# Scaling the turned features by the modulation in place of the projection weights, with a new order of the opening, row-split runs for the output projection's remainder and a last product in halves

## The chip, the cores and the metric

The kernel runs on one core of one Trainium2 chip. The metric is the device time of one execution in microseconds (us); medians over several executions are given with their lowest and highest value. The profile is one execution taken by the hardware profiler; its "span" runs from the first to the last instruction and is some 2 us shorter than the device time. The engines are called TensorE (PE in the profile, PEld for its weight loads), VectorE (DVE), ScalarE (ACT), GpSimd (POOL) and SyncE (SP, which issues DMA here).

## The reference

One layer on 2048 rows of 576 features: linear attention with 32 heads of 18, then a feed-forward part of width 4608, both behind a layer norm that is scaled and shifted by a modulation computed from a vector `c`.

```python
mod = (silu(c) @ w_mod).reshape(1, 6, 1, -1)
sa, ca, ga, sb, cb, gb = ...                     # six rows of 576
h = layernorm(x) * (1 + ca) + sa
x = x + ga * A(h)
h = layernorm(x) * (1 + cb) + sb
x = x + gb * (relu(h @ w1) @ w2)

def A(x):
    q, k, v = split(x @ wqkv)                    # 32 heads of 18
    phi_q = concat(softmax(q @ w_phi), softmax(-q @ w_phi))
    phi_k = concat(softmax(k @ w_phi), softmax(-k @ w_phi))
    kv, z = phi_k^T v, sum(phi_k)
    return (phi_q kv / (phi_q z + 1e-6)) @ wo
```

## The kernel before

Time passes in two parts. The **opening** computes the modulation, multiplies ("folds") the K and Q weights with `w_phi`, projects 16 row tiles to K, V and Q, sums kv, and runs attention for the first two tiles. Its instructions are written in one hand-searched list of short words. `Ka0` is four of the five chunks of the K projection of tile 0, `sa`/`sp` are statistics, `fs` and `ws` scale folded or value weights by `1 + ca`, `tp` forms a third of a weight difference for the feed-forward part, `nu`/`nO` are attention's numerator and its division, `W` is the output projection.

```python
ORDER = """
Z11 sx sd rp sc FK ca Z2 fs0 fsr frr fra2 sh frd4 fra0 fra1 bn1 fs3 bn0 fs1 Z1 fra3 shc sa0 wsd2 KR:0 fsd4 fs2
sp0 bn2 T0:2 VR:1 KRh bn3 Tc0 Ka0:2 KRd sa2 wsd1 ...
... Q3:0 tp0 wo4 qt1 kz Q4:1 eQ3 wo2 sq2
tp2 Q5:2 eQ4 sq3 tp1 wo3 nu0:3 eQ5 Q6:0 sq4 nO0 ...            # cut
"""
```

The **blocks**, eight of two row tiles each, run the feed-forward part: the first layer in three groups, then the second layer as seven products on sums and differences of halves (fewer multiplications than eight). Attention for the next block is slipped in: numerator in the first layer, output projection, norm and a DMA transposition in the second.

```python
def wo_mm(t, pr, add_x):
    for k in range(2):
        if add_x:                                 # the residual, through an identity matmul
            pe.matmul(pr[:, k, 0:HD], lhsT=ident[:, 0:P], rhs=x_sb[:, t, k * HD:(k + 1) * HD], start=True, stop=False)
        for ci in range(NC):                      # 5 chunks; the last has 64 real rows
            pe.matmul(pr[:, k, 0:HD], lhsT=oT[:, t % 2, ci, :], rhs=wo_sb[:, ci, k * HD:(k + 1) * HD], ...)

def l1_rest(js, u, hb):                           # half-height products, two row halves side by side
    for n, j in enumerate(js):
        for hf in range(2):
            b0 = 64 * hf
            pe.matmul(..., lhsT=w1b[b0:b0 + 64, j * P:(j + 1) * P], rhs=hb[b0:b0 + 64, 4, :], ...)

def l2(b, hooks):                                 # cut
    prod(Y, A12, B21, al, True)
    fin(t, 0, Y, 0)                               # VectorE add, GpSimd gate and residual
    if b > 0:
        pool.tensor_tensor(out=A12, in0=A12, in1=U2, op=ALU.subtract)
    ...
    prod(Z, A12, B22, al)                         # last block
    dve.tensor_tensor(out=yt[:, 0, :], in0=PS[:, Z, 0:HD], in1=gb_row[:, HD:D], op=ALU.mult)
    dve.tensor_tensor(out=x_sb[:, t, HD:D], in0=yt[:, 0, :], in1=z, op=ALU.add)
    sp.dma_start(outf[rows, HD:D], x_sb[:, t, HD:D])

def in_l1(g, u):
    if (g, u) in ((0, -1), (0, 1)):               # softmax of the query tile, and its transposition
        q_fin(q)
    if (g, u) in ((1, 2), (2, 1)):
        num_mm(t, pr); num_o(t, pr); turn_dma(oT[:, t % 2], o_sb[:, t % 2, :])

def in_l2(pos):
    if pos in (1, 4):                             # wo_mm, residual, statistics
        ...
    if pos in (2, 6):                             # normalize to xn, transpose by DMA into h2
        ln2_rs(t); ln2_apply(t, None); turn_dma(h2[...], xn[:, t % 2, :])
    if pos == 12:                                 # scale and shift the next block's features
        for ci in range(NC):
            dve.tensor_scalar(out=hb[:, ci, :], ...)
```

The softmax here doesn't subtract the row's maximum and nothing guards it: scores larger than these inputs give would overflow.

## Time and profile before

| | before |
|---|---|
| median of the first runs | 392.11 us (391.75 to 392.55, 3 runs) |
| execution that was profiled | 392.93 us, span 390.7 us |
| first feed-forward product | 93.52 us |
| each of the seven block periods | 37.05 us |
| last matmul ends | 386.79 us, tail 3.91 us |

The times of a profile are to be read from the span's start. Two markers carry most of this document: the start of the first feed-forward product (the length of the opening) and the distance between first products of neighbouring blocks (the period). What remains is the tail, from the end of the last matmul to the end of the span. The execution that was profiled was slower than every other run of that first set.

### The profile page before, as it was taken

The page shows a single profiled execution, that of the slowest core. Times are in us where ns is not written, and L with a number is a line of the kernel's source. Part 1 is how long each engine was busy: PE and PEld are TensorE (multiplying, and loading weights), DVE is VectorE, ACT ScalarE, POOL GpSimd, SP SyncE. Part 2 cuts the span into 40 slices and gives each one's busy share as a digit, 9 for nine tenths or more (in the row PEclk, how much of TensorE's full clock was granted, in tenths as well). Part 3 has the DMA queues.
Part 4 walks back from the last instruction along what each step waited for, and adds up shares of the span by engine and source line. Part 5 has one row for each costly group of instructions (what it writes and reads, how often), then busy time and mean ns, then how long its engine had stood idle before and what let it go on. Part 6 is the DMA issues. An engine that isn't in the chain of part 4 may idle for free.

```text
span 390.7 us, 8908 instructions
## 1 busy us (share of the span) xinstructions
PE 383.8 (98%) x3693; PEld 311.7 (80%) x3693; DVE 244.3 (63%) x452; ACT 157.9 (40%) x360; POOL 142.3 (36%) x199
## 2 busy tenths in 40 slices
PE   8999999999999999999999999999999999999995
PEld 4778888878887888788888878887888788878874
DVE  0889998854879746573755567458555664653221
ACT  1798779699531233124213510531143123312510
POOL 2155858741101510740164045306510641072045
PEclk9999999999999999999999999999999999999999
DMA  7999739795732151125313311450143124010001
GB/s 291 418 420 403 274 133 354 178 306 161 189 65 35 47 121 20 35 61 109 35 27 83 80 35 32 107 65 19 47 93 35 24 69 51 18 34 33 3 0 32
DMA packets 49515, 44.36 MB, mean 114 GB/s; under 512 B 39361, under 2 KB 42050, under 8 KB 48706
## 3 DMA queue, kind: packets, MB, share of 16 engines
q1 hardware_dynamic: 49186, 43.59, 39.6%
q8 instruction: 29, 0.48, 0.5%
q10 hardware_dynamic: 288, 0.19, 0.2%
q14 instruction: 12, 0.10, 0.1%
HBM read 27.97 MB, written 6.49 MB: 88 GB/s over the span
## 4 chain that ended last, share of the span: by engine, by line
PE 86%; POOL 6%; ACT 2%; DVE 2%; DMA 2%; issue 1%; SPq 0%; POOLq 0%; DVEq 0%; ACTq 0%
PE PS L683 33%; PE PS L742 29%; PE PS L274 9%; PE PS L410 5%; PE PS L690 5%; POOL wo_sb L637 2%; PE PS L235 2%; PE PS L391 1%; ACT RT L279 1%; POOL RH L754 1%; DMA gatd<-gt 1%; PE PS L324 1%; POOL RT L291 1%; DMA ga_row<-gatd 1%; DVE st L240 1%
## 5 line engine op out<-in xcount | busy, mean ns | idle before, releaser
L683 PE MATMUL PS<-h,R 128*128 128x256 bf16 x1152 | 133.5, 273 | 0.0
L683 PEld LDWEIGHTS <-R 128*128 128x128 bf16 x1152 | 109.8, 98 | 17.5 <-issue 5.1
L742 PEld LDWEIGHTS <-RH 128*128 128x128 f16 x864 | 84.5, 98 | 21.8
L728 POOL TENSOR_TENSOR yt<-yt,gb_row 128x288 f32<-128x288 f32 x23 | 16.8, 731 | 167.0 <-DVE yt L727 167.0
L742 PE MATMUL PS<-R,RH 128*128 128x288 bf16 (+1 forms) x576 | 75.6, 286 | 0.0
L697 ACT ACTIVATE RH<-PS 128x256 f16<-128x256 f32 x72 | 27.7, 384 | 114.0 <-PE PS L690 107.4
L699 DVE SCALAR_TENSOR_TENSOR RH<-PS,RH 128x256 f16<-128x256 f32 x72 | 30.1, 419 | 68.2 <-ACT RH L697 68.2
L279 ACT ACTIVATE RT<-PS,rs 128x576 bf16<-128x576 f32 x64 | 43.0, 750 | 7.5 <-PE PS L274 7.1
L698 ACT ACTIVATE RH<-PS 128x512 f16<-128x512 f32 x72 | 42.9, 595 | 7.8 <-PE PS L683 6.5
L746 ACT ACTIVATE RS<-PS 128x288 f32<-128x288 f32 x24 | 9.9, 411 | 75.9 <-PE PS L742 75.9
L742 PE MATMUL PS<-RT,RH 128*128 128x288 f16 x288 | 37.9, 286 | 0.0
L274 PE MATMUL PS<-RH,R 116*128 116x288 bf16 x240 | 31.8, 286 | 0.5 <-ACT RH L631 0.5
L754 POOL TENSOR_TENSOR RH<-RH,RT 128x2304 f16<-128x2304 f16 x7 | 31.8, 4548 | 0.0
L274 PE MATMUL PS<-RH,RT 116*128 116x288 bf16 x240 | 31.7, 286 | 0.0
L274 PEld LDWEIGHTS <-R 116*128 116x128 bf16 x240 | 22.9, 98 | 6.4 <-issue 0.7
L274 PEld LDWEIGHTS <-RT 116*128 116x128 bf16 x240 | 22.7, 98 | 5.5
L420 DVE TENSOR_SCALAR xn<-x_sb,mv,rs 128x576 bf16<-128x576 bf16 (+1 forms) x28 | 22.4, 842 | 7.3 <-ACT rs L415 7.3
L729 POOL TENSOR_TENSOR x_sb<-yt,x_sb 128x288 bf16<-128x288 f32 x31 | 22.8, 737 | 5.9 <-DVE yt L725 4.1
L240 DVE BATCH_NORM_STATS2 st<-x_sb 128x6 f32<-128x288 bf16 x60 | 24.2, 445 | 0.5
L410 PE MATMUL PS<-wo_sb,oT 128*128 128x288 bf16 x160 | 22.6, 286 | 0.2 <-POOL wo_sb L637 0.2
L284 DVE TENSOR_REDUCE Rk<-RT 128x64 f32<-128x1152 bf16 x16 | 21.2, 1332 | 1.4 <-ACT RT L279 1.4
L284 DVE TENSOR_REDUCE Rq<-RT 128x64 f32<-128x1152 bf16 x16 | 21.5, 1342 | 0.0
(115 smaller groups left out, 414.2 us busy)
## 6 DMA issues: line engine op xcount, KB each, us to landing
R<-in_w1a_dram SPq DMA_DIRECT2D x4, 1152.0 KB
eqd<-RT SPq DMA_DIRECT2D x14, 288.0 KB, 5.8
RT<-eqd SPq DMA_DIRECT2D x14, 288.0 KB, 2.7
R<-in_w2a_dram SPq DMA_DIRECT2D x3, 864.0 KB, 10.4
R<-in_w2b_dram SPq DMA_DIRECT2D x2, 1296.0 KB, 10.9
out_dram<-x_sb SPq DMA_DIRECT2D x15, 144.0 KB, 3.3
RT<-in_xT_dram SPq DMA_DIRECT2D x2, 640.0 KB
x_sb<-in_xk_dram SPq DMA_DIRECT2D x3, 288.0 KB
```

Source lines behind the costliest of these rows:

```text
L240: dve.bn_stats(out=s[:, hf, :], in_=x_sb[:, t, hf * HD:(hf + 1) * HD])
L274: pe.matmul(pr[:, k, 0:HD], lhsT=xt(t, ck), rhs=w[0:R, ck, k * HD:(k + 1) * HD], start=(ck == 0), stop=(ck == NC - 1))
L279: act.activation(out=E.rearrange("p (b h s e) -> p b h s e", b=2, s=2, e=DH)[:, :, :, s, :], in_=pr[:, :, 0:HD].rearrange("p b (h e) -> p ...
L284: dve.tensor_reduce(out=Rr, in_=E.rearrange("p (c e) -> p c e", e=DH), axis=AXX, op=ALU.add)
L410: pe.matmul(pr[:, k, 0:HD], lhsT=oT[:, t % 2, ci, :], rhs=wo_sb[:, ci, k * HD:(k + 1) * HD], start=(ci == 0 and not add_x), stop=(ci == NC ...
L683: pe.matmul(PS[:, 2 * u + hf, n * 256:n * 256 + 256], lhsT=w1a[:, ci, jj * P:(jj + 1) * P], rhs=hb[:, ci, :], start=(n == 0 and ci == 0), ...
L697: act.activation(out=A11[:, j, :], in_=lo[:, :, 0, :], func=ACT.Relu)
L698: act.activation(out=A2[:, j, :, :], in_=PS[:, 2 * u + 1, :].rearrange("p (n s f) -> p n s f", n=2, s=2), func=ACT.Relu)
L699: dve.scalar_tensor_tensor(out=U3[:, j, :], in0=lo[:, :, 1, :], scalar=0.0, in1=A11[:, j, :], op0=ALU.max, op1=ALU.subtract)
L729: pool.tensor_tensor(out=x_sb[:, t, c], in0=y, in1=x_sb[:, t, c], op=ALU.add)
L742: pe.matmul(PS[:, bank, 0:HD], lhsT=am[:, j, :], rhs=bm[:, j, :], start=first and j == 0, stop=(j % 9 == 8), skip_group_check=True)
L754: pool.tensor_tensor(out=A12, in0=A12, in1=U2, op=ALU.subtract)
```

## The change

The intent is fourfold. (1) In the opening the weights stay raw; instead the transposed features are multiplied by `1 + ca`, pair by pair, on three engines, so the first K projection waits for less; the loads and the whole order are searched anew. The residual is added by VectorE and not by identity matmuls. (2) In blocks with index 2 and more, attention moves to an earlier place, and the output projection's fifth chunk runs as two half-height products side by side, next to other such products. (3) GpSimd's subtraction for the last product moves to VectorE, except in the block with index 1. (4) The very last product is computed in halves of 144 columns.

```diff
+    def x_scale(t, eng):                         # in place of f_scaled, wv_scale, FQs
+        for ck in range(NC):
+            v, f = xt(t, ck, 2), ca1[0:R, ck:ck + 1]
+            act.activation(out=v, in_=v, func=ACT.Copy, scale=f)      # or VectorE; GpSimd all at once
-        "W": lambda i: wo_mm(i, at["W", i], True), "lb": lambda i: ln2_bn(i, at["W", i]), ...
+        "W": lambda i: wo_mm(i, at["W", i]), "xr": lambda i: add_res(i, at["W", i]), "lb": lambda i: bn(1, i), ...
 ... (the ORDER list and the order of the loads are new throughout)
         fin(t, 0, Y, 0)
         if b > 0:
-            pool.tensor_tensor(out=A12, in0=A12, in1=U2, op=ALU.subtract)
+            (pool if b == 1 else dve).tensor_tensor(out=A12, in0=A12, in1=U2, op=ALU.subtract)
 ... (last block)
-        prod(Z, A12, B22, al)
-        dve.tensor_tensor(out=yt[:, 0, :], in0=PS[:, Z, 0:HD], in1=gb_row[:, HD:D], op=ALU.mult)
-        dve.tensor_tensor(out=x_sb[:, t, HD:D], in0=yt[:, 0, :], in1=z, op=ALU.add)
+        for i, bank in enumerate((Z, 0)):
+            c, g = slice(i * H4, (i + 1) * H4), slice(HD + i * H4, HD + (i + 1) * H4)
+            for j in al:
+                pe.matmul(PS[:, bank, c], lhsT=A12[:, j, :], rhs=B22[:, j, c], ...)
+            dve.tensor_tensor(out=yt[:, 0, c], in0=PS[:, bank, c], in1=gb_row[:, g], op=ALU.mult)
+            dve.tensor_tensor(out=x_sb[:, t, g], in0=yt[:, 0, c], in1=yl[:, c], op=ALU.add)
+    def wo_rest(t, pr):
+        for k in range(2):
+            b0 = 64 * k
+            pe.matmul(pr[:, k, 0:HD], lhsT=oT[b0:b0 + 64, t % 2, 4, :], rhs=wo_sb[b0:b0 + 64, 4, ...], ...)
 ... (in_l1, in_l2: blocks 0 and 1 keep the old places, from index 2 on)
+            if (g, u) in ((0, 0), (0, 2)):
+                attend(t0 + u // 2)
+            if g and u == "rest":
+                wo_rest(t0 + g - 1, pair(3))
+            if g and u == 0:
+                wo_full(t, pair(3)); add_res(t, pair(3)); bn(1, t)
+            if b > 1 and pos in (4, 10) or b == 1 and pos == 8:
+                q_next(t0 + 2 + pos // 8)         # softmax of a query tile, now in the second layer
```

## The prediction

> **What bounds the kernel now.** I read the page first: shares by engine, then the chain of waits.
>
> ```profile
> span 390.7 us, 8908 instructions
> PE 383.8 (98%) x3693; PEld 311.7 (80%) x3693; DVE 244.3 (63%) x452; ACT 157.9 (40%) x360; POOL 142.3 (36%) x199
> ...
> PE 86%; POOL 6%; ACT 2%; DVE 2%; DMA 2%; issue 1%; SPq 0%; POOLq 0%; DVEq 0%; ACTq 0%
> ```
>
> TensorE is busy for 98% of the span and carries 86% of the last chain. But matmuls overlap, so busy time is no proof that the rate is full. I therefore went to the chain in order of time for one feed-forward block (there are eight, 37.05 us apart) and compared pieces with counts.
>
> ```profile
> 130.73 3.06 PE PS L683 x28
> 133.79 0.76 PE PS L690 x12
> 134.55 5.35 PE PS L683 x48
> 139.90 0.76 PE PS L690 x12
> 140.66 2.29 PE PS L683 x20
> 142.95 0.38 PE PS L391 x10
> ...
> 149.81 1.19 PE PS L742 x9
> 151.00 1.23 PE PS L410 x10
> 152.22 3.31 PE PS L742 x27
> 155.53 1.23 PE PS L410 x10
> 156.76 11.03 PE PS L742 x90
> ```
>
> First number start, second length. 90 second-layer products take 11.03 us, 122.6 ns each; 28 first-layer products 3.06 us, 109 ns; the 12 half-height ones 0.76 us, 63 ns each, because they run in pairs. All pieces touch. Adding the pieces of one block gives 3 x 6.11 (first layer) + 2 x 0.38 (attention numerator) + 2 x 1.23 (output projection) + 126 x 0.1226 = 37.0 us, which is the period. So the blocks, from 93.5 us to the end, have no gap: only fewer or cheaper matmuls help there.
>
> The opening is different. The TensorE timeline before 24 us has waits and fill-in matmuls on zeros:
>
> ```profile
> 12.58 0.38 PE L235 MATMUL PS<-zero 128*128 128x512 bf16 x1
> 12.79 0.38 PE L251 MATMUL PS<-siluc,R 116*116 116x1 bf16 x5
> 13.04 0.38 PE L235 MATMUL PS<-zero 128*128 128x512 bf16 x1
> 14.16 1.40 PE L268 MATMUL PS<-R,RS 116*100 116x288 bf16 x10 [0.75 <-DVE RS L614]
> ...
> 19.62 0.27 PE L577 MATMUL PS<-ident,sc 128*100 128x128 bf16 x2 [0.26 <-DVE RH L481]
> ...
> 23.41 1.39 PE L274 MATMUL PS<-RH,R 116*128 116x288 bf16 x10 [0.49 <-ACT RH L631]
> ```
>
> The brackets name who was waited for. The shift copy (L614) sits behind statistics on VectorE; the correction row (L481) behind weight scalings. VectorE is busy 10.2 of the 10.6 us from 14.16 to 24.72. The first K projection starts at 16.74. Summing real work from 14.16 to 93.52 at its pitch (480 projections x 0.1226 = 58.9, 24 output products 2.9, rows 2.5, folds 1.7, kv 5.8, gates and modulation 2.6, transposes and numerators 2.8) gives 77.2 us of 79.4, so some 2.2 us of gaps, half before 24.72. Last, the end of the kernel:
>
> ```profile
> 377.93 4.54 POOL L754 TENSOR_TENSOR RH<-RH,RT 128x2304 f16<-128x2304 f16 x1
> ...
> 386.89 0.46 DVE L777 TENSOR_TENSOR yt<-PS,gb_row 128x288 f32<-128x288 f32 x1 [1.75 <-PE PS L742]
> 387.49 0.46 DVE L778 TENSOR_TENSOR x_sb<-yt 128x288 bf16<-128x288 f32 x1
> 387.98 0.33 SPq L779 DMA_DIRECT2D out_dram<-x_sb  x1
> ```
>
> The last matmuls end at about 386.8; two VectorE operations of 0.46 and the store follow. GpSimd's late chain (the 4.54 us subtraction, then gate and residual) ends at 387.46 and holds the second one by about 0.1.
>
> **What the Trainium skill says.** "TensorE: Matmul & The Clock Gate", section "Wait — 56ns, not 53.3ns?", gives a warm back-to-back pitch of N / 2.4 GHz + 2.5 ns: 122.5 ns for 288 columns, 109.2 for 256. The trace agrees (122.6 and 109). "TensorEngine Tiling (Array Packing)", section "Key Properties", says that independent row tiles can run in parallel and that changing the tiling mode drains the engine. The trace agrees with the first: twelve half-height products are six slots of 0.107 = 0.64 us, and take 0.76; the 0.12 left is what I take for the switch. So adding a pair to a run that is already split should cost one slot and no switch. "VectorE: DVE Perf Modes", section "The perf-mode tier table (the rule you actually need)", puts a 16-bit tensor-scalar from on-chip memory at four elements a cycle and anything from PSUM at two at most; here 116x576 scaled from SBUF took 366 ns and the 116x504 scaling from PSUM 0.73 us, so it agrees.
>
> **The change, part by part.**
>
> 1. Feature scaling in place of weight scaling, with the new order. Off VectorE go five value-weight scalings at a pitch of 0.31 (1.55 us), one 0.65 and one 0.44 fold scaling; off ScalarE four fold scalings of 0.69 and five query-fold ones of 0.73 (6.4 us). New: eight pairs of tiles must be scaled, five 116x256 slices each on VectorE (two pairs) and ScalarE (three), one 116x1280 multiply on GpSimd (three). From the 335 ns row for 128x256 on VectorE I take at most 0.3 a slice, 1.3 us a pair. ScalarE: the 4x256 copy's 0.38, 1.7 to 1.9 us a pair. GpSimd: 576 elements took 1.17 to 1.27, so 1280 about 2.7. These lie mostly beside TensorE. What counts is the start: the K projection no longer waits for the correction rows; its first four chunks need raw folded weights, scaled features and the modulation scale. The new load order delivers in sequence at about 0.4 MB/us (725 + 288 + 725 + 725 + 320 KB plus the small ones), so the features land near 11.4; scale ready at 9.5, copies done near 12, shift products done near 12.9. Ka0 can start near 13 instead of 16.74, but rows, fill-ins and the two last chunks then follow. Laying them end to end, the pair of K tiles is complete at about 18.3 instead of 19.2, and four later projections end near 22.9 instead of 24.6. I take 1.4 us saved at the start, and 0.4 of the later gaps.
>
> 2. Residual added on VectorE, not by identity matmuls: 4 x 0.1226 = 0.49 us of TensorE gone. VectorE pays 2 x 0.75 instead; ScalarE loses two 0.65 copies. The path to the first block's features gets longer, but Q projections lie beside it. Saved: 0.45.
>
> 3. Output projection's remainder in row-split runs, in blocks with index 2 to 6, two tiles each. Ten matmuls per tile become eight full plus one concurrent pair: 10 x 0.1226 - (8 x 0.1226 + 0.1226) = 0.123 us. Ten tiles: 1.2 us, all on TensorE's full path.
>
> 4. Subtraction for the last product moved from GpSimd (4.5 us) to VectorE (about 1.36) in most blocks: no matmul waits on it now, so nothing, except that the last block's GpSimd chain ends earlier (0.1).
>
> 5. Last product in halves of 144 columns: matmul time is the same (36 x about 0.061 against 18 x 0.1226), but the closing two VectorE operations work on half as much. From 0.46 at 288 wide to about 0.31 each, 0.3 saved, with the 0.1 above 0.4.
>
> Zero products (24 in both kernels) stay. Sum: 1.4 + 0.4 + 0.45 + 1.2 + 0.4 = 3.85, taken from the measured 392.1 (not the span): about 388.2.
>
> **The rivals.** *GpSimd and VectorE become the opening's bound.* From 24.7 to 60 us VectorE is busy 32.4 of 35.3 and GpSimd 23.8; two or three scalings of 2.7 each push GpSimd above 29, and its K-minus step feeds the value path. For it: little slack. Against: TensorE shows no gap there now, several tiles are in flight. It would give back 1 to 2 us, ending at 389 to 390. *The opening is bound by loads:* the share of DMA is 1.02 from 14 to 25 us, and the features come after two weight blocks; were the first K projection held until 14, the start would gain nothing: 389.5. *A new wait in the blocks:* attention, transposes through DMA (2.6 us from issue to landing, issues of 1.2 or more on one queue) and the residual now share the first layer. The first tile's transpose is asked for about 6 us into a block and wanted near 10.7; about 1 us of slack. A miss of 0.5 in five blocks would eat the 1.2 and more: about 391. *A better opening:* if all gaps after a start at 13 closed, up to 4 us would go there instead of 1.8: 386.
>
> **Range and chances.** 388.2 us; the size of the opening gain is my weakest number, the row split and halves are counted. Range 385.9 to 390.2. Two per cent is 7.8 us, twice my sum and more than all visible gaps plus all removed matmuls (about 2.2 + 1.7 + 0.4 + 2 at the start), so faster by over 2% gets 0.04; slower would need stalls in every block: 0.01. Within 2%: 0.95.
>
> **What would show it.** In the new profile: the first feed-forward product near 91.2 instead of 93.52; blocks 2 to 6 (those before the last that hold the projection) with a period of 36.8 instead of 37.05, the split run there 0.12 longer and the two projections shorter by 0.245 each; a tail after the last matmul near 3.5 instead of 3.9; first K projection near 13. I am wrong if the projection after a split run shows a wait for the transposed attention output, if ScalarE or GpSimd scalings appear as TensorE's releasers between 25 and 60 us, or if the period does not drop.

## The result and the profile after

The kernel after takes 392.01 us in the median (391.89 to 392.08, 4 runs), the kernel before beside it 392.23 us (391.75 to 392.55, 4 runs). The ratio is 0.9994 with a 95% interval of 0.9979 to 1.0009. Ratios here are the mean time of one kernel's runs over that of the other's of the same rounds, so they are not quite the ratio of the medians. Executions over 1.5% slower than the fastest of the same kernel are left out of the means. The predicted 3.9 us are missing and the time lies above the range. The head of its page:

```profile
span 390.2 us, 8945 instructions
PE 382.7 (98%) x3707; PEld 310.3 (80%) x3707; DVE 244.4 (63%) x469; ACT 157.5 (40%) x376; POOL 126.6 (32%) x196
...
PE 90%; DMA 3%; DVE 2%; ACT 2%; issue 2%; POOL 1%; SPq 0%; POOLq 0%; DVEq 0%
```

TensorE holds a larger share of the last chain than before, and GpSimd's share fell from 6% to 1%; yet DMA rose from 2% to 3%, of which 1% is the transposition of the blocks' features. These shares do not tell where the time went. The markers do:

| | before | before, second profile | after | after, second profile |
|---|---|---|---|---|
| first modulation product | 6.39 | 6.15 | 5.99 | 6.08 |
| first K projection | 16.74 | 16.11 | 12.49 | 12.56 |
| first product of the kv sums | 24.72 | 24.10 | 24.83 | 24.80 |
| first feed-forward product | 93.52 | 93.00 | 93.60 | 93.58 |
| periods of blocks 0, 1, 2 | 37.05 each | 37.05 each | 37.20, 37.05, 37.56 | 37.22, 37.05, 37.41 |
| periods of blocks 3 to 6 | 37.05 | 37.05 | 36.71 to 36.72 | 36.71 |
| first feed-forward product to last matmul | 293.27 | 293.27 | 292.63 | 292.50 |
| tail | 3.91 | 3.93 | 3.97 | 3.92 |

**The opening did start earlier.** In the TensorE timeline of the kernel after (start us, length us, engine, line, operation, tiles and shapes, count, and in brackets the wait and whom it was for), the third line is the product for the correction rows, which now follows the first K projection:

```profile
8.51 1.60 PE L434 MATMUL PS<-RS,R 126*116 126x126 bf16 x25 [0.27 <-DMA R<-in_wkT_dram]
...
12.49 1.15 PE L272 MATMUL PS<-RH,R 116*128 116x288 bf16 x8
13.48 1.39 PE L266 MATMUL PS<-RH,RS 116*100 116x288 bf16 x10
```

At the first product of the kv sums the new order has done one V projection (ten matmuls, 1.23 us) more than the old one. For equal work the old order stands at 24.72 + 1.23 = 25.95 in the first profile and at 25.33 in the second, so the lead is 1.1 or 0.5 us. **Then it was lost**: from there to the first feed-forward product the old order needs 68.80 - 1.23 = 67.57 us, the new one 68.77, although four identity matmuls (0.49) are gone. The largest single piece stands in the chain of waits of the kernel after (start, length, what):

```profile
75.75 2.00 DVE RT L465 x2
...
79.01 0.36 DVE rden L396
...
79.39 0.77 DVE o_sb L397
...
80.20 0.45 PE PS L524 x5
```

The first two pieces of weight difference (L465, for the feed-forward part later) stand on VectorE ahead of attention's division for tile 0 (L396, L397), and the transposition of its result on TensorE (L524) waits. Counting each matmul at its usual pitch, TensorE has 1.12 us of gaps between 60 us and the first block, 0.72 of them here, where the kernel before had 0.36 in all.

The old order has its three pieces (L474 there) ahead of the division as well, and VectorE takes as long over them. The second profile of the kernel before, in which TensorE came earlier than in the first, shows the same wait of its transposition (L529):

```profile
74.03 3.60 DVE L474 TENSOR_TENSOR RT<-R 128x1728 f16<-128x1728 bf16 x2
...
77.93 0.76 DVE L399 TENSOR_TENSOR o_sb<-PS,rden 128x576 bf16<-128x576 f32 x1
...
78.74 0.45 PE L529 MATMUL PS<-ident,o_sb 128*128 128x128 bf16 x5 [0.28 <-DVE o_sb L399]
```

TensorE's gap here is 0.45 us; in the first profile it was none, because TensorE itself was not ready before 78.92. So this wait is no fault of the new order alone.

**The blocks** got shorter from index 3 on by 0.34 us each, which is what the row split was for, and longer at the head of the block with index 2. **The end** did not move against the last matmul. The timeline of the kernel after:

```profile
385.44 0.74 POOL L720 TENSOR_TENSOR x_sb<-yt,x_sb 128x288 bf16<-128x288 f32 x1
...
386.21 0.31 DVE L776 TENSOR_TENSOR yt<-PS,gb_row 128x144 f32<-128x144 f32 x1 [1.67 <-POOL x_sb L720]
...
387.46 0.33 SPq L778 DMA_DIRECT2D out_dram<-x_sb  x1
```

The multiply of the first closing half writes the buffer `yt` that GpSimd is still reading for another tile, so it waits (the bracket), and both halves end up behind the last matmul, which ends at 386.23. The last store is issued 1.23 us after it; before it was 1.19.

### The profile page after: what moved, and what is told of

Its sections match the earlier page's. It is cut to its first block, busy times and chain, and to the rows that moved or that the text cites. A ratio compares the mean times of both kernels' runs of the same rounds, so it can differ in the third digit from the quotient of the medians.

```text
span 390.2 us, 8945 instructions
## 1 busy us (share of the span) xinstructions
PE 382.7 (98%) x3707; PEld 310.3 (80%) x3707; DVE 244.4 (63%) x469; ACT 157.5 (40%) x376; POOL 126.6 (32%) x196
## 4 chain that ended last, share of the span: by engine, by line
PE 90%; DMA 3%; DVE 2%; ACT 2%; issue 2%; POOL 1%; SPq 0%; POOLq 0%; DVEq 0%
PE PS L673 33%; PE PS L733 28%; PE PS L272 13%; PE PS L680 5%; PE PS L806 3%; PE PS L406 2%; DMA R<-in_wkT_dram 2%; PE PS L389 1%; PE PS L322 1%; DMA h<-xn 1%; PE PS L249 1%; ACT RT L277 1%; DVE RT L465 1%; ACT RT L511 0%; PE PS L434 0%
## 5 line engine op out<-in xcount | busy, mean ns | idle before, releaser
L673 PEld LDWEIGHTS <-R 128*128 128x128 bf16 x1152 | 111.0, 98 | 16.0 <-issue 2.8
L733 PEld LDWEIGHTS <-RH 128*128 128x128 f16 x846 | 82.8, 98 | 20.8
L719 POOL TENSOR_TENSOR yt<-yt,gb_row 128x288 f32<-128x288 f32 x23 | 23.1, 1003 | 192.3 <-DVE yt L718 192.3
L733 PE MATMUL PS<-R,RH 128*128 128x288 bf16 (+1 forms) x558 | 72.4, 286 | 0.0
L689 DVE SCALAR_TENSOR_TENSOR RH<-PS,RH 128x256 f16<-128x256 f32 x72 | 29.0, 414 | 64.5 <-ACT RH L687 64.5
L238 DVE BATCH_NORM_STATS2 st<-x_sb 128x6 f32<-128x288 bf16 x64 | 26.0, 448 | 5.1 <-DMA x_sb<-in_xk_dram 4.6
L272 PEld LDWEIGHTS <-R 116*128 116x128 bf16 x240 | 22.9, 98 | 6.9 <-issue 1.4
L718 DVE TENSOR_TENSOR yt<-PS,RS 128x288 f32<-128x288 f32 x23 | 10.4, 453 | 26.2 <-PE PS L733 21.0
L282 DVE TENSOR_REDUCE Rq<-RT 128x64 f32<-128x1152 bf16 x16 | 21.5, 1341 | 1.3 <-ACT RT L277 1.3
L680 PE MATMUL PS<-h,R 64*128 64x256 bf16 x288 | 19.9, 271 | 0.0
L411 DVE TENSOR_TENSOR x_sb<-x_sb,PS 128x576 bf16<-128x576 bf16 x16 | 12.1, 754 | 12.2 <-PE PS L806 8.1
```

The source lines that it names most:

```text
L238: dve.bn_stats(out=s[:, hf, :], in_=x_sb[:, t, hf * HD:(hf + 1) * HD])
L272: pe.matmul(pr[:, k, 0:HD], lhsT=xt(t, ck), rhs=w[0:R, ck, k * HD:(k + 1) * HD], start=(ck == 0), stop=(ck == NC - 1))
L282: dve.tensor_reduce(out=Rr, in_=E.rearrange("p (c e) -> p c e", e=DH), axis=AXX, op=ALU.add)
L673: pe.matmul(PS[:, 2 * u + hf, n * 256:n * 256 + 256], lhsT=w1a[:, ci, jj * P:(jj + 1) * P], rhs=hb[:, ci, :], start=(n == 0 and ci == 0), ...
L680: pe.matmul(PS[:, 2 * u + hf, n * 256:n * 256 + 256], lhsT=w1b[b0:b0 + 64, j * P:(j + 1) * P], rhs=hb[b0:b0 + 64, 4, :], start=False, stop ...
L689: dve.scalar_tensor_tensor(out=U3[:, j, :], in0=lo[:, :, 1, :], scalar=0.0, in1=A11[:, j, :], op0=ALU.max, op1=ALU.subtract)
```

## The experiments

All kernels gave correct results, except the one that was made wrong. "The change" below is the kernel after.

### Is the stall at the head of block 2 a matter of the blocks or of the opening?

Edit: the kernel before with its old opening, and the new blocks and the new ending.

```diff
 # before.py, opening unchanged
-    (l1_rest ... in_l2 of before)
+    (l1_rest ... in_l2 of the change, with wo_rest, wo_full, norm2, q_next)
+    wo[D:] = g["A_wo"][512:]
```

> The old opening with only the new feed-forward blocks and the new ending. Theory (the blocks gain by themselves, the opening gave nothing): block period 36.72 us for blocks 3 to 6 as in the changed kernel, 37.05 for blocks 0 and 1, and time equal to the changed kernel's 392.0 within 0.4, since both openings reach the first block at 93.5 to 93.6. Rival (the new blocks only keep pace because the new opening leaves something ready, or the stall before block 2 is caused by the new opening): no stall of 0.9 us before block 2 here, time near 391.1.

Measured: 391.24 us (390.61 to 391.51, 6 runs), ratio 0.9973 (0.9962 to 0.9985). The block periods are 37.05, 37.06, 37.31 and then 36.71. So the stall comes with the new blocks, in a smaller size. The time lies below the band that I had set. The first feed-forward product, at 93.11, is as in the second profile of before: I had taken the first profile of before, with its 93.52, as the rule, and it was not. The three profiles of the old opening start the kv sums at 24.72, 24.10 and (here) 23.87, but the first division of the attention ends at 78.81, 78.69 and 78.80 in all of them: a lead was lost in the old order too. Ahead of the division two pieces of weight difference lie beside GpSimd's scaling of the output weights and take 3.09, 3.60 and 3.93 us together; a piece alone takes 1.05. That GpSimd holds them up was not tested by itself.

### Does the row split pay what was counted?

Edit: both half-height products of the output projection on the same row half, so that they cannot run side by side (the number of matmuls is the same; both row halves hold the same data).

```diff
-lhsT=oT[b0:b0 + 64, t % 2, 4, :], rhs=wo_sb[b0:b0 + 64, 4, k * HD:(k + 1) * HD]
+lhsT=oT[0:64, t % 2, 4, :], rhs=wo_sb[0:64, 4, k * HD:(k + 1) * HD]
```

> The two half-height products of the output projection both on rows 0 to 63, so that they cannot run side by side; all else as in the changed kernel, result right. Theory (concurrency is what saves): each pair takes 0.24 instead of 0.12 us, period of blocks 3 to 6 rises from 36.72 to 36.96, time 1.2 us longer than the changed kernel. Rival (the saving comes from where the projection was moved to, fewer drains): period stays within 0.05 of 36.72.

Measured: 393.23 us (392.98 to 393.42), ratio 1.0025 (1.0013 to 1.0037). Periods 36.95 in place of 36.71 from block 3 on. Its chain of waits shows the pair (L800):

```profile
215.50 0.76 PE PS L680 x12
216.26 0.24 PE PS L800 x2
```

In the change the same two take 0.12. The loss of 0.24 a block, about 1.2 us in five (the trace shows it plainly in the four from block 3 on; block 2 has the stall besides), shows up nearly whole in the time: the blocks are on the path and the row split is worth what was predicted.

### Do the weight differences ahead of the division cost time?

```diff
-... qt1 tp1 Q6:1 eQ5 wo1 qi2 tp0 nu0:2 eQ6 Q7:3 sq5 nO0 wo3 sq4 nu1:0 tp2 eQ7 ot0:1 sq6 Q8:2 nO1 w2b1 ...
+... qt1 Q6:1 eQ5 wo1 qi2 nu0:2 eQ6 Q7:3 sq5 nO0 wo3 sq4 nu1:0 eQ7 ot0:1 sq6 Q8:2 nO1 tp1 tp0 tp2 w2b1 ...
```

> The three weight differences on VectorE moved behind the attention of the first two tiles. Theory (the opening's end is held by VectorE's order: two differences of 1.71 us sit ahead of the first attention division, and TensorE waits 0.72 us for it at 79 us): this gap falls under 0.1, first block starts at 92.9 instead of 93.6, time 0.7 shorter. Rival (the attention's transposes through DMA, wanted at 77.5, or the chain behind hold it anyway): the gap moves to the second tile or to the residual, start stays within 0.2 of 93.6.

Measured: 391.31 us (390.87 to 391.36, 5 runs), ratio 0.9973 (0.9961 to 0.9985). The first feed-forward product starts at 92.86. The timeline shows that VectorE now idles until the numerator is ready and divides at once:

```profile
77.88 0.36 DVE L396 RECIPROCAL rden<-PS 128x32 f32<-128x32 f32 x1 [2.04 <-PE PS L389]
78.27 0.76 DVE L397 TENSOR_TENSOR o_sb<-PS,rden 128x576 bf16<-128x576 f32 x1
```

In the new order this one misplacement cost 0.7 us (whether the old order escapes it, see the pair of runs with all repairs). In its place ahead of the division, 1.71 us apiece, the weight differences also ran beside GpSimd's scaling of the output weights; here, later, they take 0.99.

### Does a buffer of their own let the closing halves overlap?

```diff
+    ye = RE[:, 2 * HD:4 * HD].bitcast(FP32)
-            dve.tensor_tensor(out=yt[:, 0, c], in0=PS[:, bank, c], ...)
-            dve.tensor_tensor(out=x_sb[:, t, g], in0=yt[:, 0, c], in1=yl[:, c], op=ALU.add)
+            dve.tensor_tensor(out=ye[:, c], in0=PS[:, bank, c], ...)
+            dve.tensor_tensor(out=x_sb[:, t, g], in0=ye[:, c], in1=yl[:, c], op=ALU.add)
```

> The two closing half operations write a buffer of their own, not the one that GpSimd still reads for the other tile. Theory (the halves' gain was lost to a write-after-read wait on GpSimd, 1.67 us before the first half): the first half's multiply starts near 385.1 rather than 386.2, only the second half stays behind the last matmul, span 0.5 shorter, time near 391.5. Rival (the final store is bound by the queue, with two earlier stores of 0.3 to 0.4 just ahead of it): the last store is issued under 0.2 earlier and the time stays at 392.0.

Measured: 391.98 us (391.63 to 392.08), ratio 0.9992 (0.998 to 1.0004): no gain to be seen, so a miss. The wait went (the multiply starts at 385.14, once its product is done), but the add behind it lasts 0.79 instead of 0.31, up to just behind the end of GpSimd's operation beside it:

```profile
385.44 0.73 POOL L721 TENSOR_TENSOR x_sb<-yt,x_sb 128x288 bf16<-128x288 f32 x1
385.55 0.79 DVE L778 TENSOR_TENSOR x_sb<-RE 128x144 bf16<-128x144 f32 x1
```

The last store is issued at 387.10 in place of 387.46; such 0.36 us drown in the spread of the runs (0.45 here).

### How far do two runs of the same kernel differ?

Edit: none; the change and the kernel before were each run and profiled again.

> The changed kernel once more, unaltered, beside the kernel before on the chip of the next three. Theory: 392.0 as in its first timing, ratio 0.9985 to 1.000, so that the old opening with the new blocks (391.2, ratio 0.997) was truly faster than the whole change. Rival (chip to chip scatter made that difference): ratio 0.997 or lower.

> The kernel before, unaltered, once more with a profile. Theory (its first profile caught a late weight load: first modulation product at 6.39 us, against 5.93 in two later runs with the same opening): the first modulation product comes at 5.9, the first block starts near 92.7 instead of 93.52, span near 389.9. Then the new opening (93.6) is slower by some 0.8 than the old one. Rival (the first profile was typical): start at 93.5 again.

Measured: the change 391.78 us (391.7 to 391.92), ratio 0.9988 (0.9973 to 1.0003); the kernel before 391.97 us (391.86 to 392.41), ratio to its other runs 0.9991 (0.9974 to 1.0007). The markers of the change agree within 0.15 us. Those of before do not: its opening stands at 93.00 in place of 93.52; the first modulation product started at 6.15 and not at 6.39 and the correction rows at 13.54 and not at 14.16. The very start differs: the twelve fill-in matmuls ahead of that product took 5.30 us in the first profile, 4.64 in this one and 4.20 in the version with the new blocks, which started it at 5.93. What I expected, 92.7, was a little too far. The starting point of my prediction was thus half a microsecond late, and as much of the gain that I read off it was not there to be had.

### Is GpSimd's subtraction in block 1 behind the stall?

```diff
-            (pool if b == 1 else dve).tensor_tensor(out=A12, in0=A12, in1=U2, op=ALU.subtract)
+            dve.tensor_tensor(out=A12, in0=A12, in1=U2, op=ALU.subtract)
```

> In block 1 the subtraction for the last product on VectorE, as in the later blocks, not on GpSimd. Theory (GpSimd's 4.5 us subtraction slows VectorE's normalization of the next tile from 0.64 to 2.88 us, so its transposes land late and TensorE waits 0.9 us at the head of block 2): normalization back to 0.64, landing about 1 us earlier, no stall, block 2 starts at 168.0, time 0.9 shorter. Rival (the stall is of the extra attention-input work put before the scaling in that block): stall stays above 0.6.

Measured: 391.64 us (391.29 to 392.2, 6 runs), ratio 0.9986 (0.9974 to 0.9999). The period of block 2 falls to 36.72: the stall is gone, and block 3 starts 0.7 us earlier. The timelines show how; first the change:

```profile
158.06 4.54 POOL L745 TENSOR_TENSOR RH<-RH,RT 128x2304 f16<-128x2304 f16 x1
160.10 2.88 DVE L420 TENSOR_SCALAR xn<-x_sb,mv,rs 128x576 bf16<-128x576 bf16 x2 [1.21 <-ACT rs L415]
...
166.89 2.34 DVE L857 TENSOR_SCALAR h<-h,mod 128x256 bf16<-128x256 bf16 x5 [0.51 <-DMA h<-xn]
```

and the version with the subtraction on VectorE:

```profile
160.19 0.64 DVE L420 TENSOR_SCALAR xn<-x_sb,mv,rs 128x576 bf16<-128x576 bf16 x2 [0.60 <-ACT rs L415]
...
166.37 1.77 DVE L857 TENSOR_SCALAR h<-h,mod 128x256 bf16<-128x256 bf16 x5
```

The normalization (L420) lasts 2.88 us beside GpSimd's subtraction and 0.64 without it. The transposition by DMA behind it, and the scaling of the next block's features (L857), come 2.2 us and 0.5 us earlier. The device time fell by less than the 0.7 of the trace; the tail of the profiled execution was 4.34 us, and at its end the closing multiply waits longer for GpSimd (2.03 us, 1.67 in the change), so that the last store is issued only 0.40 earlier.

### Why then did the kernel before not stall?

The timeline of the kernel before, for the same block, shows the same collision:

```profile
157.83 4.55 POOL L754 TENSOR_TENSOR RH<-RH,RT 128x2304 f16<-128x2304 f16 x1
159.86 2.89 DVE L420 TENSOR_SCALAR xn<-x_sb,mv,rs 128x576 bf16<-128x576 bf16 x2 [1.21 <-ACT rs L415]
...
166.06 1.78 DVE L820 TENSOR_SCALAR h<-h,mod 128x256 bf16<-128x256 bf16 x5
```

So the long normalization cannot be the whole cause. Before, the last of the five feature scalings ends at 167.84 and the next block's first product starts at 167.62: there was no slack left, but no stall either. The change adds to the same stretch the softmax work of a query tile (1.34 + 0.35 us on VectorE, 0.25 + 1.17 on GpSimd), and its transposition landed 3.7 us after its issue and not 2.6. Two more edits ask about this. The first moves the query work of block 1 behind the feature scaling:

```diff
-            if b > 1 and pos in (4, 10) or b == 1 and pos == 8:
+            if b > 1 and pos in (4, 10) or b == 1 and pos == 13:
```

> The changed kernel with one edit: in the second block the softmax work of the query tile for the block after is moved from position 8 to position 13 of the second layer, behind the scaling of the features for the next block; GpSimd's subtraction stays where it is. The profile of the kernel before has the same long normalization (2.89 us beside a 4.55 us GpSimd operation) and no stall, so that cannot be all of the cause. Theory C (the added query work takes the slack: 1.34 + 0.35 us on VectorE, 1.4 on GpSimd, which push GpSimd's gate and residual beside the feature scaling, 2.34 instead of 1.78): the feature scaling is back at 1.78, the stall ahead of the third block is 0.3 or less, unless the numerator of the next block then waits for its query tile. Rival D (the normalization and the late landing of the transposition, 3.7 instead of 2.6 us, make the stall): landing still above 3.4 and a stall of 0.4 or more. Time about 391.5 under C, 392.0 under D.

Measured: 394.13 us (393.32 to 395.28), ratio 1.0058 (1.0033 to 1.0084). The head of block 2 is clean: the 28 first products start at 168.19, a period of 37.06 behind the one before, and show no wait, although the normalization still takes 2.89 us and the transposition still lands after 3.8. The five scalings now take 1.37 us together. So theory C holds for the head of the block. Its proviso came true as well: the query tile is late, the numerator waits 0.44 for it and the output projection's half-height pair 1.41 for the transposed attention output, so the period of block 2 grows to 38.92. At the one other place that was tried the query work thus cost more; a third place was not tried.

The second edit asks whether VectorE is slowed beside GpSimd or held until GpSimd is done. GpSimd's subtraction is issued ahead of the gate and residual:

```diff
+        if b == 1:
+            pool.tensor_tensor(out=A12, in0=A12, in1=U2, op=ALU.subtract)
         fin(t, 0, Y, 0)
-        if b > 0:
-            (pool if b == 1 else dve).tensor_tensor(out=A12, in0=A12, in1=U2, op=ALU.subtract)
+        if b > 1:
+            dve.tensor_tensor(out=A12, in0=A12, in1=U2, op=ALU.subtract)
```

> The changed kernel with one edit: in the second block (index 1) GpSimd's subtraction for the last product is issued ahead of the gate and residual of the first closing quarter instead of behind them, so it should run from about 156.5 to 161.1 us instead of 158.1 to 162.6. Theory A (the VectorE normalization beside it does not run slowly but waits until GpSimd's operation ends): the second normalization of that block, start about 160.1, ends at about 161.5 instead of 163.0, so its pair lasts about 1.3 instead of 2.88, the transposition is asked for 1.5 us earlier and the stall ahead of the third block goes (period of block 2 near 37.05 or 36.75 instead of 37.4 to 37.6). Rival B (the normalization is slowed by a factor all the time it lies beside GpSimd work): it still lasts over 2 us and the stall stays above 0.3. Time about 391.3 under A, 391.9 under B.

Measured: 392.57 us (392.51 to 392.95), ratio 1.0014 (0.9999 to 1.0029), so the gain that I expected is a miss: now the other tile's normalization was caught, and everything behind it came later; the stall grew to two waits of 0.38 and 0.42. But the mechanism shows clearly in the timeline:

```profile
155.49 4.93 DVE L420 TENSOR_SCALAR xn<-x_sb,mv,rs 128x576 bf16<-128x576 bf16 x2
...
155.85 4.54 POOL L744 TENSOR_TENSOR RH<-RH,RT 128x2304 f16<-128x2304 f16 x1 [2.18 <-PE PS L733]
```

VectorE's pair ends at 155.49 + 4.93 = 160.42, GpSimd's operation at 155.85 + 4.54 = 160.39. With 0.63 us of own work, the pair was held until GpSimd was done: one of its two operations alone took 4.59 us. This agrees with the Trainium skill, "SBUF — State Buffer", section "Who interferes with whom": of a VectorE operation in a two-port mode and a GpSimd operation, the one that is issued first has the shared ports for its whole length, and the other "fully blocks". Which was issued first is not to be read here, as the two start within about 0.02 us; in the change GpSimd was first, by 2.04. The trace of the change agrees too: there the pair of normalizations ends at 162.98, 0.38 after GpSimd's subtraction.

### What do the feature scalings cost?

Edit, wrong result: the six scalings on ScalarE and GpSimd do nothing.

```diff
-"xp": lambda t: x_scale(t, pool), "xa": lambda t: x_scale(t, act),
+"xp": lambda t: None, "xa": lambda t: None,
```

> Feature scaling left out for all tile pairs from 4 on (a wrong result on purpose); the first two pairs keep theirs. Theory (the scalings on ScalarE and GpSimd, 2.1 to 2.3 us each, delay the exponentials and value path, which gives the gaps of 0.8 us between 37 and 46 us): these gaps fall under 0.2, first block starts at 93.0 rather than 93.7, time 0.7 shorter. Rival (VectorE's sums and statistics are the cause there, or the end of the opening takes back what is won): start stays within 0.2 of 93.7.

Measured: 391.63 us (391.27 to 391.77, 4 runs), ratio 0.9983 (0.997 to 0.9996). Two gaps of TensorE ahead of 41.6 and 45.4 us, 0.26 and 0.18, are gone, and the stretch from the kv sums to the first block is 68.38 in place of 68.77. The kv sums themselves start later here (25.11), after a wait for VectorE at 21.5 us, so that the first block comes only 0.1 earlier, at 93.49. The three gaps between 36.7 and 38 us stay, so they are not of the scalings' making. The rival "scalings bound the opening" is right for some 0.4 us, no more.

### Three repairs together, and how much the new opening is worth

Edit of the first: the whole change with the three repairs above (weight differences later, block 1's subtraction on VectorE, own buffer for the closing halves). Edit of the second: the same blocks, ending and repairs with the old opening.

```diff
 # the change, or the old opening with the new blocks
+ weight differences behind nO1
+ dve.tensor_tensor(out=A12, ...)      # every block
+ ye in place of yt                    # closing halves
```

> The whole change with the three repairs: weight differences behind the first attention, block 1's subtraction on VectorE, a buffer of its own at the end. Theory (repairs add up, and the new opening is the slower one): first block at 92.9, no stall at block 2, time 390.5 to 390.9, so 0.2 to 0.5 above the old opening with the same repairs (390.53). Rival (the new opening is equal once repaired): 390.2 or less.

> The old opening with the new blocks, with the weight differences behind the first attention, block 1's subtraction on VectorE and a buffer of its own for the end. Theory (all three repairs add up and the old opening costs nothing): opening gap of 0.78 at 78 us gone, stall of 0.6 before block 2 gone, end 0.35 shorter; against the run with only the new blocks (391.2) 1.5 us shorter, 389.7, ratio 0.993 to 0.994. Rival (the repairs collide with the old order or the end hides them): 390.5 or more.

Measured: with the new opening 390.02 us (389.78 to 390.33, 6 runs), ratio 0.9939 (0.9926 to 0.9952); with the old one 390.53 us (390.28 to 390.78, 4 runs), ratio 0.9956 (0.9943 to 0.9969). The first is the best version: 2.2 us below the 392.24 of before beside it, where the change as it stood gave 0.2. The theory that the new opening is the slower one fell by time: the two intervals overlap and the new opening has the lower median. By the markers it is not faster, though: its first feed-forward product is at 92.79, the old one's at 92.27; the tails were 3.61 and 4.69. From the last matmul to the issue of the last store both take the same (0.88 and 0.87), so the old one's longer tail arises after that, and why was not found. What the new opening alone is worth is therefore not settled by these two runs: half a microsecond in its favour by the time, half a microsecond against it at the first block.

The two runs settle another question. In the old order the move of the weight differences shortened the stretch from the kv sums to the first block from 69.24 us (the version with only the new blocks) to 68.44, in the new order from 68.77 to 67.96 alone and 67.99 here. It is worth 0.8 in both, so it does not tell the orders apart.

Together the repairs gave 2.0 us, more than their single results add up to (about 0.7, 0.15 to 0.4, and none). The markers account for it: against the change the first feed-forward product comes 0.81 earlier, the blocks are 0.83 shorter and the tail 0.36. Alone, the subtraction's move gained 0.84 in the blocks too, but lost part of it in its tail of 4.34; a likely reason for the difference is the own buffer. The pairs of repairs were not run.

### Could the old opening take the identity matmuls' removal, or the new one other repairs?

Four edits, each to one wait that the timeline showed.

```diff
 # e9_noid: e7_oldbest with the residual on VectorE
-... W0:3 eQ9 sq7 lb0 ... W1:1 ap0 eQ10 sq9 lb1 xc0 ...
+... W0:3 eQ9 xr0 sq7 lb0 ... W1:1 ap0 eQ10 sq9 xr1 lb1 ...
 # e10_shc: e9_noid with the shift copy ahead of statistics
-bn1 fs3 bn0 fs1 Z1 fra3 shc sa0
+bn1 fs3 fs1 Z1 fra3 shc bn0 sa0
 # e11_xa: e8_newbest with a ScalarE scaling later
-FQ4:0 xa12 pA4 ... eK6 sK7
+FQ4:0 pA4 ... eK6 xa12 sK7
 # e12_t2: e8_newbest with the second pair's row transposition ahead of the value rows
-KRd1 Kb0 VR:1 ... VRh1 T2:0 Z2 VRh0 Tc2 ...
+KRd1 T2:3 Kb0 Tc2 VR:1 ... VRh1 Z2 VRh0 ...
```

> The old opening with the repaired new blocks, and of the new opening only the residual on VectorE in place of four identity matmuls. Theory (this part is worth its count, 4 x 0.1226 = 0.49 us, since TensorE is full at the end of the opening): 390.0 to 390.1. Rival (VectorE's two additions of 0.75 lengthen the path to the first block's features and TensorE waits for them): 390.5 or more.

> As the one before, with the copy of the shift ahead of one tile's statistics in VectorE's order. Theory (the gap of 0.87 us before the correction rows is this copy's place in the order): rows start 0.6 to 0.8 earlier, time 0.5 less than the one before. Rival (VectorE is full in these 10 us, so the wait only moves to the correction rows or the first K tiles): first block within 0.2 of the one before.

> The repaired whole change, with ScalarE's scaling of the fourth pair (tiles 12 and 13) moved behind the exponentials of tiles 7 and 6. Theory (its 2.1 us in front of them held back their banks and caused the gaps of 0.26 and 0.18 at 41 to 43 us): from the start of the kv sums to the first block 0.4 less than the repaired change's 68.0 us, time 0.4 less than 390.0. Rival (the scaling delays whatever comes after it): the gaps move to the next K tiles, same time.

> The repaired whole change, with the transposition of the second statistics pair and its copy moved ahead of the value rows. Theory (TensorE waits 0.45 us at 18.5 us, beside 0.43 of fill-ins, for a copy that stands behind the value rows' copies on ScalarE): the next K projection starts at 18.5 instead of 19.2 and the first block 0.4 earlier. Rival (the exponentials of tile 0 or the value rows then hold the following projections): first block within 0.2.

Measured: 390.85 us (ratio 0.996), 391.09 us (0.9968), 391.3 us (0.9975) and 390.38 us (0.9952). None beats the version it started from (390.53 for the first, the first itself for the second, 390.02 for the last two); the first and the last are within the intervals of theirs. Each removed what it aimed at and raised a wait elsewhere. Without the identity matmuls, in the old order, the first block starts at 93.08 in place of 92.27: the transposition of the first block's features waits 0.53 us for VectorE's normalized features, and the projection behind it 0.35 for ScalarE. With the copy moved, a product behind it waits 0.35 for GpSimd. With the scaling moved, two gaps of 0.26 and 0.18 went, and this one came in the TensorE timeline:

```profile
46.74 0.53 PE L272 MATMUL PS<-RH,R 116*128 116x288 bf16 x3 [1.51 <-DVE RT L303]
```

because the scaling now stood on ScalarE ahead of the normalizer of the same tile. With the transposition moved, the next K projection started at 18.77 in place of 19.16, a fold behind it then waited 0.46 for ScalarE, and the first feed-forward product stood at 92.79 as before. In the opening, gaps are kept by several engines at once; taking one wait away at its place seldom shortens the whole.

## Why the prediction was wrong

Most of the counts were right; the sum of 3.85 us was not, and here is each of its terms.

**Start of the opening, 1.4 predicted.** The first K projection at 12.49 was as foreseen ("near 13"). The lead at the kv sums was 1.1 us against the profile that I had read, 0.5 against a second one and 0.3 against the version with the new blocks (23.87 + 1.23 = 25.10). Two steps failed. I took one profile's start as given: the execution was 392.93 us long where the median was 392.1, and I had both numbers before me. And I laid the later projections end to end, four of them by 22.9. They end near 24.7 in the change: the pair of K tiles is complete at 18.0, as foreseen, but the next projection waits until 19.15 for a copy on ScalarE, and shorter waits follow. (The old order had three by 24.6, not four.)

**"0.4 of the later gaps".** This step failed with the wrong sign. In place of a gain, 1.69 us were lost between the kv sums and the first block, counted beside the 0.49 of removed matmuls: 67.57 - 0.49 = 67.08 us for the same work in the old order, 68.77 in the new. Against the other two profiles of the old opening it is 1.59 and 1.25. The weight differences ahead of the division are the largest single wait, but the old order has them too and gains as much without them. With them moved in both orders, the new one is still behind by 67.99 - (68.44 - 1.23 - 0.49) = 1.27. Counted at the usual pitch, five gaps of TensorE in the new order make this up: 0.45 in two, which the run without scalings took away, so 0.4 for the scalings is shown; some 0.5 in three at 36.7 to 38 us; and 0.3 at 79 us, ahead of the second tile's numerator. The last two are read in the timeline but were not tested, so some 0.8 of the loss has a place and no shown cause. My argument against the rival had been that TensorE "shows no gap there now, several tiles are in flight". It spoke of the old order; a new order has new gaps, and I had no means to see them.

**Identity matmuls, 0.45 predicted.** Four matmuls did go. In the new order the saving is part of the sum above and cannot be told apart; in the old order, where it was tried alone, the time did not fall and the first block came 0.81 later: the step that "Q projections lie beside" the longer path did not hold there, for TensorE waited for VectorE and ScalarE.

**Row split, 1.2 predicted: right.** Undoing it cost 0.24 us a block and 1.2 us in all against the change. The late blocks even gained 0.34 each instead of 0.245; about 0.1 a block is left over that I did not isolate.

**"No matmul waits on it now, so nothing."** This was said of GpSimd's subtraction, and it holds for the product that the subtraction feeds. The step overlooked that the subtraction also holds VectorE's normalization beside it until it ends, and that the change left it on GpSimd in just the block in which it put query work into the second layer. Block 2 has a period of 37.56 and not 36.71: 0.85 us lost (0.70 in the second profile). Two things make it together: the held normalization, which the kernel before had too, and the added query work; taking away either by itself clears the head of the block. With the old opening, where the transposition landed after 2.6 us, the loss was there but smaller, 0.6, so the later landing probably makes the rest. I had named the rival "a new wait in the blocks" but looked for it at the transposed attention output, where it appeared only in the experiment that moved the query work. In block 0 a further 0.16 was lost in the first stretch of products.

**Closing halves, 0.4 predicted: 0.** The multiply and add took 0.31 each, as estimated, but the first half's multiply waits for GpSimd's read of the same buffer until 386.21, so the halves run one behind the other after the last matmul. With a buffer of its own the wait went, and the last store was issued 0.36 earlier, close to the term, yet the time of that run hardly moved. The step overlooked which buffer GpSimd still had to read.

**The sum.** Against the first profile of before: opening +0.1, blocks -0.64, tail +0.06, which is a span shorter by 0.5. The second profiles of both: opening +0.6, blocks -0.77, tail 0, which is 0.2 shorter. The measured ratio of 0.9994, 0.2 us of 392, is of this size. One reading of the prediction is too strong besides: 366 ns for 576 elements and 0.73 us for 504 show that the scaling from PSUM is about half as fast as the one from on-chip memory, but not the rates of four and two elements a cycle.

## What to carry to other kernels

Before estimating what an earlier start is worth, follow it to the next point at which all engines meet; a lead that is not carried there can be lost in the order of work that comes next. Two operations on VectorE and GpSimd that share nothing in the program can still hold each other up: look for an operation whose length in the trace is several times its usual one, and compare its end with the end of the other engine's operation. And take the starting point of a small estimate from two profiles rather than one, above all where the profiled execution is not near the median.

## What the Trainium skill lacked or had wrong

- "GPSIMD Engine Reference", section "1. Specifications": its table calls the sharing with VectorE "contention", which reads like a slowdown. Here the loser stopped: a pair of normalizations of 0.63 us took 4.93 us and ended 0.03 us after GpSimd's operation. The page on SBUF has this right.
- "TensorEngine Tiling (Array Packing)", section "Key Properties": it says that a change of tiling mode drains the engine but gives no cost. Here twelve half-height products side by side take 0.76 us where six slots of 0.107 would be 0.64, and a pair added to such a run costs 0.12 us, its slot alone, against 0.24 when both lie on the same rows. So about 0.1 us goes with the run and not with its pairs; that it is the drain was not tested.
- No page that I found says how much a DMA transposition's landing varies. In all profiles of the old opening it is 2.6 us; in all of the new opening the longest of fourteen took 3.4 to 4.2 us. In the windows that I looked at, a 0.02 MB packet of the instruction queue moved at the same time. That it is the cause was not tested.
